# Attention with block summaries and two MLPs on one core: second batch's v means from one product, first heads whole, a new order and engine table

## The chip, the cores and the metric

The kernel runs on one core of one Trainium2 chip, as one program. The metric is the device time of that core in microseconds (us). Three runs of the kernel before took 600.23, 600.83 and 600.94 us, a median of 600.83. Five engines work side by side: TensorE (PE, with its weight loads as PEld), VectorE (DVE), ScalarE (ACT), GpSimd (POOL) and SyncE (SP), which here only issues transfers. Each runs its own list of instructions in order and waits on semaphores for the others.

## What is computed

```
q, k, v: (2, 8, 768, 64)         block, window = 32, 16
k_sum = max  of k over each block of 32 tokens      -> (B, H, 24, D)
v_sum = mean of v over each block of 32 tokens      -> (B, H, 24, D)
scores_l = q k^T / 8, masked to |i - j| < 16
scores_s = q k_sum^T / 8 + log(32)
a   = softmax over [scores_l, scores_s]
out = a @ [v, v_sum]                                -> x: (1536, 512)
x   = MLP 1: h = x @ w_in (512 x 2048), g = rational(h), x = g @ w_out
out = MLP 2: h = x @ w_in (512 x 2048), g = h cos(h),    out = g @ w_out
```

The weights come as 64-bit floats and are converted on the chip.

## The kernel before

The tokens of both batches are cut into 12 units of 128 tokens, six for each batch. A unit u goes through three steps. `attn_a` gathers the 96 keys of each half's window beside the 24 block maxima into a tile `kw` (in `room`), makes the scores of all 8 heads in two PSUM tiles (`sp`, 16 products of 120 columns), and then does the softmax head pair by head pair: DVE adds the mask and finds the maximum (line 656), ACT takes the exponential (660), DVE inverts the sums (670), POOL or DVE scales (673). `attn_b` transposes the scaled scores (`ptp`, line 687) and copies them out (`pt`). `attn_c` multiplies them with a tile `vw` that holds 96 rows of v and 24 rows of block means (`avp`, line 734); its result becomes two halves of x (`xH`, and `xL` on line 745).

The block means of v are a product too. Tokens are loaded with 2 per partition, DVE or POOL adds the pairs, and a product with the selector `vsel` (1/32 where a partition belongs to a block) sums the rest. A batch has 768 tokens, so it takes 3 loads, 3 additions and 3 products of 512 columns that add up in one PSUM bank (`vmp`): `v_mean0` (lines 507, 514, 517) for batch 0 and `v_mean1` (loads of `raw`, lines 539 and 542) for batch 1. The result is copied to `big`, and four small transfers (line 719) bring it to the four `vw`.

Batch 0's keys come as 8 loads into `part` and are transposed by products (`ktp`, line 463); each is copied (327) and reduced to maxima (471). The queries of units 0 and 1 come as two loads, one for each 4 heads, and are transposed in halves (`qtp`, line 432). For units 0 and 1 `attn_a` works head pair by head pair: four gathers, four groups of 4 products, each with its own waits.

The MLPs follow in the same stream of PE work: `h` products (864, later 962), elementwise work on ACT, DVE and POOL, `acc` products (1106). Weight tiles of 512 KB come into `raw`, a pool of 3 buffers that `v_mean1` shares, and DVE converts each with three instructions (760, 764, 768), the last of which frees the buffer. Their loads all start at line 415.

The order is fixed. `Plan.op` records every operation with the engines that may run it, and `Plan.order` reads the packed table `ORDER`, which gives the place of each operation in one long list and its engine. Every engine gets its operations in that sequence, and SP its transfers. PSUM has 4 shared banks (`ps`) and 4 accumulators (`acc0` to `acc3`, used early for transposes).

Of the kernel before, what the change touches and what calls it, by code (L numbers as in the profile page):

```python
# [35 lines left out]
for _p, _t in (("AA", .143), ("AP", .17), ("AT", .25), ("AV", .14), ("PA", .08), ("PP", .08), ("PT", .15),  # L36
# [20 lines left out]
    "c-rk)ON?g6RsQOA-*w;jf4}<g{`)o4-P7Zq=^1+-9?wi>?7=wWB#vccTP8ROa%>aJ1|csTD`5dy#8QX>i%1qqK!CD{;t"  # L57
    "+(8B3OY4Qp5_0B|FwE*dTFk)xEbTSwz6PtN-r*KB~^+JKs5{sv+FasgQC63MdEQF^-Fy3?2?-dffr`rQ~1-$In5*agKK"
    "P57-&k`|Y{do&Zb5F~_gT=?vlcRZ+5_?~j0?E?gY!IH~l<s?;B1UKL`F0`eH%5ZANt0$7PXEnM*sR~{H}mI<6w-*>?BU"
    "w4xwmORI7%gcCzc#wUS>jW~_#U#^V`a~lC>24UnzonvA;c_U3vv1$SRovaZeVJXy^`Cy~^7auPd1?!nzJ6uv@y&<NZ+`"  # L60
    "8Mw>ED=A3eIk&ttiDaG*BVw$I@F;>PaIx39muxxd(Y=ffW@HdYHP=iglW=6rGZjrshU!{-h@eK^1J)ZxJ;>_7368{+8j"
    ";MSXm&dxp_+y1F~VQ}RqJI|~Bz0Y2LM!ga|T|Iqw?QV7VBG$@s?fO*Ct8sCCRP10l$glL5`LcI>+{@=xKAj$y<^JJ442"
    "v6sb9=~xtzMO2RSc6Kt}pU9E@x@~;ZeNX8$zF1@9S!JQQShgm`$%0FJ5&gSr!hCqgxkK#9{Hc#z7R^O2XaUca;9zPVn+"
    "p^l0R7JpZRF1n$~7S3bSkd}@AX-`(4t&1Ro~bL%Z^+<cSYxcBykb1fFvL>3L>FGhL%imPtCER!-(;%xSs*cCfa{A(X<d"
    "g8s5_j%-%-1A5L?PpzGI68Qv;K_hXeaHXH@@B+^P~KIcxqE>hE%+By@KrAu&v@`c>GHvEMcR8f{LCf~qoI10$!O&sF4<"
    "IUs)<-%jThqm#g6mLXzPn?_B;HQ1^=%R=d2j@er2!s8J4|G4El1h`^K5#e2&%n{=aR;>)6(d|JYjm%PQWO|2q~5J|7(c"
    "!GA7334h=*jEZvb&&U;IMnrlfj=_n}=lu!?z>~Lg=Mkh^Th7g^|A0qVa3X=r9J2rsyud+NIS#x?UI>q3In*8iAG^qyix"
    "ohc_#rr4?9#L!QvwP64RLw?SHQ;~<KrLb+xY%1Y=18VR)3D_&)6s3?@(qqA2|ysJ-ZDV4j_VlZ4)x2xEx22tOu`p%)3!"
# [173 lines left out]
def pool(n):  # L242
    return Shared(0.2 + n * 0.00207)
# [7 lines left out]
def kernel(  # L251
# [92 lines left out]
    NQ, NVW = 2, 4  # L344
    NKW = 2
# [154 lines left out]
    def v_mean0(lead):  # L500
# [3 lines left out]
        for i in range(3):  # L504
# [11 lines left out]
            P.op([("T", 0.89)], [raw], [vp],  # L516
# [12 lines left out]
    def v_mean1(lead):  # L529

        kr = kT[1]
        o2 = NP * S + NP * NB
        vp = psum([128, NH, D], "vmp")
        for i in range(3):
            raw = load([128, NH, 2 * D], F32, "raw", "raw", 3,
                       v[1, :, 256 * i:256 * i + 256, :].rearrange("h (s j) d -> s h (j d)", j=2),
                       lambda t: t, 1.75, P.now - lead)
            P.op([("P", pool(512)), ("V", dve2(512))], [], [raw],
                 lambda e, raw=raw: E[e].tensor_tensor(
                     out=raw.t[:, :, 0:D], in0=raw.t[:, :, 0:D], in1=raw.t[:, :, D:2 * D], op=ALU.add))  # L540
            P.op([("T", 0.89)], [raw], [vp],
                 lambda e, i=i, raw=raw: nc.tensor.matmul(  # L542
                     out=vp.t[WK:KW], lhsT=vsel[:, 16 - 8 * i:40 - 8 * i], rhs=raw.t[:, :, 0:D],
                     start=i == 0, stop=i == 2))
        P.op([("A", act(512, True)), ("V", dve(512))], [vp], [kr["v"]],
             lambda e: cp(e, kr.t[WK:KW, o2:o2 + NH * D].rearrange("p (h d) -> p h d", h=NH), vp.t[WK:KW]))
        P.now += 2.7
# [3 lines left out]
    def q_tile(u, lead):  # L551
        b, t = divmod(u, UPB)
        tp = psum([128, NP, 128], "qtp", u < 2)
        if u == 0:
            for i in range(2):
# [6 lines left out]
                     prio=P.now - lead)  # L562
        dst = qTs[u % NQ]
        if u < 2:
            for i in range(2):
                def tr(e, i=i):
                    for x in range(2):
                        transpose_pairs(tp.t[:, 2 * i + x, :], q_first[i][1]()[:, 2 * x:2 * x + 2], 64 * u, 64)

                P.op([("T", 0.44)], [q_first[i][0]], [tp[i], dst[i]], tr)  # L570
                P.op([("A", act(256, True)), ("V", dve(256))], [tp[i]], [dst[i]],
                     lambda e, i=i: cp(e, dst.t[:, 2 * i:2 * i + 2], tp.t[:, 2 * i:2 * i + 2]))
            P.now += 0.88
            return
        raws = [load([128, NH, D], F32, "qk", "qk", 3,
                     q[b, :, 128 * t:128 * t + 128, :].rearrange("h s d -> s h d"), lambda t: t, 1.3,
                     P.now - lead)]

        def tr(e):
            for pr in range(NP):  # L580
                nc.tensor.transpose(tp.t[:, pr, :], raws[0].t[:, 2 * pr:2 * pr + 2], ident)

        P.op([("T", 0.44)], raws, [tp, dst[0], dst[1]], tr)
        P.op([("A", act(512, True)), ("V", dve(512))], [tp], [dst[0], dst[1]], lambda e: cp(e, dst.t, tp.t))
        P.now += 0.44

    def win(u):

# [738 lines left out]
```

## Time and profile before

| what | us |
|---|---|
| median of 3 runs | 600.83 |
| the profiled execution, whole | 601.26 |
| its span in the trace | 599.4 |
| PE busy | 585.9 (98%) |
| DVE busy | 548.4 (92%) |
| ACT busy | 434.1 (72%) |
| POOL busy | 304.3 (51%) |

The whole time is 1.9 us more than the span of the engines' work. The granted TensorE clock is 1.00 in every stretch. An engine's busy share is an average over unlike stages: the attention units lie in the first sixth of the span, beside the first products of MLP 1, and after that come only MLP units. The end of the program is set by the last `acc` products and their output.

### The profile page before, as it was taken

The page shows a single profiled execution, that of the slowest core. Times are in us where ns is not written, and L with a number is a line of the kernel's source. Part 1 is how long each engine was busy: PE and PEld are TensorE (multiplying, and loading weights), DVE is VectorE, ACT ScalarE, POOL GpSimd, SP SyncE. Part 2 cuts the span into 40 slices and gives each one's busy share as a digit, 9 for nine tenths or more (in the row PEclk, how much of TensorE's full clock was granted, in tenths as well). Part 3 has the DMA queues.
Part 4 walks back from the last instruction along what each step waited for, and adds up shares of the span by engine and source line. Part 5 has one row for each costly group of instructions (what it writes and reads, how often), then busy time and mean ns, then how long its engine had stood idle before and what let it go on. Part 6 is the DMA issues. An engine that isn't in the chain of part 4 may idle for free.

```text
span 599.4 us, 10933 instructions
## 1 busy us (share of the span) xinstructions
PE 585.9 (98%) x3897; PEld 501.0 (84%) x3897; DVE 548.4 (92%) x1119; ACT 434.1 (72%) x954; POOL 304.3 (51%) x303
## 2 busy tenths in 40 slices
PE   8879999999999999999999999999999999999997
PEld 7568878888888888888888888888989989998996
DVE  4999999979999999998999999999999998887874
ACT  3989999877587756876789897766767566554653
POOL 5587975247537564557577542444355423732130
PEclk9999999999999999999999999999999999999999
DMA  9897874200321313311220112123322331100104
GB/s 264 218 258 192 204 209 120 75 0 2 106 71 37 106 36 105 106 52 56 70 71 1 36 36 71 37 71 104 109 71 70 106 108 36 35 1 1 53 1 158
DMA packets 68862, 51.85 MB, mean 87 GB/s; under 512 B 37304, under 2 KB 63160, under 8 KB 68808
## 3 DMA queue, kind: packets, MB, share of 16 engines
q1 hardware_dynamic: 68664, 51.03, 29.0%
q8 instruction: 30, 0.49, 0.3%
q14 instruction: 24, 0.20, 0.1%
q10 hardware_dynamic: 144, 0.13, 0.1%
HBM read 47.71 MB, written 3.15 MB: 85 GB/s over the span
## 4 chain that ended last, share of the span: by engine, by line
PE 87%; DVE 9%; ACT 2%; DMA 1%; issue 0%; POOL 0%; SPq 0%; POOLq 0%; DVEq 0%; ACTq 0%
PE acc L1106 43%; PE h L864 22%; PE h L962 18%; DVE sc L656 2%; DMA vw<-in_v_dram 1%; PE avp L734 1%; DVE f L764 1%; DVE f L768 1%; PE ptp L687 1%; PE sp L626 1%; PE warm L356 1%; PE ktp L463 1%; DVE f L760 1%; PE vmp L542 0%; DVE big L471 0%
## 5 line engine op out<-in xcount | busy, mean ns | idle before, releaser
L1106 PE MATMUL acc<-gh,w 128*128 128x512 f32 (+1 forms) x416 | 123.1, 378 | 0.0
L1106 PE MATMUL acc<-w,gh 128*128 128x512 f32 x382 | 119.3, 394 | 0.0
L864 PE MATMUL h<-xH,w 128*128 128x512 f32 (+1 forms) x320 | 99.1, 371 | 0.1
L777 POOL TENSOR_TENSOR gl<-te,gh 128x512 fp32r<-128x512 f32 (+1 forms) x48 | 62.7, 1307 | 67.2 <-ACT gh L322 33.5
L1106 PEld LDWEIGHTS acc<-gh,w 128*128 128x128 f32 x416 | 75.3, 188 | 14.9 <-issue 1.5
L1106 PE MATMUL acc<-gl,w 128*128 128x512 f32 (+1 forms) x208 | 77.6, 373 | 0.0
L1106 PEld LDWEIGHTS acc<-w,gh 128*128 128x128 f32 x382 | 66.7, 189 | 9.4
L1106 PE MATMUL acc<-w,gl 128*128 128x512 f32 x191 | 74.3, 389 | 0.0
L1023 POOL TENSOR_TENSOR tu<-tu,tf 128x512 f32<-128x512 f32 (+1 forms) x41 | 51.4, 1255 | 41.2 <-ACT tf L1015 40.9
L777 POOL TENSOR_TENSOR w<-f,w 128x512 fp32r<-128x512 f32 x39 | 54.4, 1397 | 29.5 <-ACT w L322 15.0
L864 PEld LDWEIGHTS h<-xH,w 128*128 128x128 f32 x320 | 58.5, 188 | 10.6 <-DVE big L495 0.3
L864 PE MATMUL h<-xL,w 128*128 128x512 f32 (+1 forms) x160 | 58.9, 368 | 0.0
L864 PE MATMUL h<-big,w 128*128 128x512 f32 x216 | 52.0, 389 | 0.0
L768 DVE SCALAR_TENSOR_TENSOR f<-raw,f 128x512 int32<-128x512 int32 x64 | 48.3, 759 | 0.3
L1013 ACT ACTIVATE tu<-h,co 128x512 f32<-128x512 f32 (+1 forms) x52 | 33.9, 652 | 19.3 <-PE h L864 18.2
L764 DVE SCALAR_TENSOR_TENSOR f<-raw,f 128x512 int32<-128x512 int32 x64 | 47.3, 745 | 0.6
L864 PEld LDWEIGHTS h<-big,w 128*128 128x128 f32 x216 | 40.6, 188 | 8.4
L1106 PEld LDWEIGHTS acc<-gl,w 128*128 128x128 f32 x208 | 39.1, 188 | 7.0
L1106 PEld LDWEIGHTS acc<-w,gl 128*128 128x128 f32 x191 | 35.9, 188 | 7.9
L1057 ACT ACTIVATE tu<-te 128x512 int32<-128x512 f32 x27 | 17.1, 632 | 32.5 <-DVE te L987 32.2
L324 POOL TENSOR_SCALAR w<-f 128x512 fp32r<-128x512 f32 x28 | 20.0, 715 | 39.8 <-DVE f L768 35.1
L1033 ACT ACTIVATE h<-tf 128x512 f32<-128x512 f32 (+1 forms) x52 | 29.6, 570 | 12.0 <-DVE te L1027 10.8
(222 smaller groups left out, 1530.9 us busy)
## 6 DMA issues: line engine op xcount, KB each, us to landing
raw<-in_moe_w_in_dram SPq DMA_DIRECT2D x32, 512.0 KB, 4.6
raw<-in_moe_w_out_dram SPq DMA_DIRECT2D x32, 512.0 KB, 3.4
vw<-in_v_dram SPq DMA_DIRECT2D x24, 192.0 KB, 3.5
qk<-in_q_dram SPq DMA_DIRECT2D x10, 256.0 KB, 5.3
out_dram<-part SPq DMA_DIRECT2D x8, 256.0 KB, 2.8
part<-in_k_dram SPq DMA_DIRECT2D x8, 192.0 KB, 4.8
big<-in_v_dram SPq DMA_DIRECT2D x3, 512.0 KB, 6.7
qk<-in_k_dram SPq DMA_DIRECT2D x6, 256.0 KB, 5.4
```

The costliest lines, as they stand in the source:

```text
L324: nc.gpsimd.tensor_scalar(out=o, in0=i, scalar1=1.0, scalar2=1.0, op0=ALU.mult, op1=ALU.mult)
L656: lambda e, pr=pr, hh=hh, sv=sv, sp=sp: nc.vector.tensor_tensor_reduce(out=sv()[:, pr, :], in0=sp.t[:, pr, :], in1=m.t, op0=ALU.add, op1=A ...
L764: lambda e: nc.vector.scalar_tensor_tensor(out=ft.t.bitcast(I32), in0=lohi()[1], scalar=-0x40000000, in1=ft.t.bitcast(I32), op0=ALU.bitwis ...
L768: lambda e: nc.vector.scalar_tensor_tensor(out=ft.t.bitcast(I32), in0=lohi()[0], scalar=29, in1=ft.t.bitcast(I32), op0=ALU.logical_shift_r ...
L777: lambda e: E[e].tensor_tensor(out=lo(), in0=x(), in1=hi().bitcast(F32), op=ALU.subtract),
L864: nc.tensor.matmul(out=h.t[:, 0:n], lhsT=lt, rhs=rt[:, kk, cs], start=(k0 == 0 and i == 0), stop=(k0 == 2 and i == 5))
L962: nc.tensor.matmul(out=bank.t[:, c], lhsT=lt, rhs=rt, start=start and i == 0, stop=stop and i == 5, skip_group_check=True)
L1013: lambda e: nc.scalar.activation(out=U(), in_=H(), func=ACTF.Square, scale=b1s))
L1023: lambda e: E[e].tensor_tensor(out=U(), in0=U(), in1=Z(), op=ALU.add))
L1033: lambda e: nc.scalar.activation(out=H(), in_=Z(), func=ACTF.Exp, scale=-1.0))
L1057: lambda e: nc.scalar.activation(out=K().bitcast(I32), in_=S_(), func=ACTF.Identity, scale=1.0 / (2.0 * math.pi)))
L1106: nc.tensor.matmul(out=dst, lhsT=lt, rhs=rt, start=(un.start and not have and i == 0), stop=(un.stop and i == 2), skip_group_check=have)
```

## The change

It has three parts beside a new table.

- Batch 1's means: 4 loads of 96 partitions, each partition with 8 tokens of which a load brings 2. The pairs of each load are added, the second to fourth results are added to the first, and one product over 96 partitions with a rebuilt selector gives all 24 blocks. The selector is rebuilt on POOL after batch 0's products. The first load's `raw` buffer is held until that product.
- The heads of units 0 and 1 are whole: one transpose step and one copy for each unit's queries, one gather, one group of 16 score products, as for the other units. All keys are loaded and transposed first.
- `ORDER` gives a new sequence and new engines for operations all over the kernel.

```diff
     def v_mean1(lead):
...
-        for i in range(3):
+        def eighths(e):
+            sel = vsel[:, 0:24]
+            nc.gpsimd.memset(sel, 1.0 / 32.0)
...
+        P.op([("P", 0.6)], [], [vsel_r], eighths)
+        first = None
+        for i in range(4):
             raw = load([128, NH, 2 * D], F32, "raw", "raw", 3,
-                       v[1, :, 256 * i:256 * i + 256, :].rearrange("h (s j) d -> s h (j d)", j=2),
-                       lambda t: t, 1.75, P.now - lead)
+                       v[1].rearrange("h (s j) d -> s h (j d)", j=8)[:, :, 2 * D * i:2 * D * i + 2 * D],
+                       lambda t: t[0:NW8], 1.13, P.now - lead)
...
             P.op([("P", pool(512)), ("V", dve2(512))], [], [raw],
...
-            P.op([("T", 0.89)], [raw], [vp],
-                 lambda e, i=i, raw=raw: nc.tensor.matmul(
-                     out=vp.t[WK:KW], lhsT=vsel[:, 16 - 8 * i:40 - 8 * i], rhs=raw.t[:, :, 0:D],
-                     start=i == 0, stop=i == 2))
+            if first is None:
+                first = raw
+                continue
+            P.op([("P", pool(512)), ("V", dve2(512))], [raw], [first],
+                 lambda e, raw=raw: E[e].tensor_tensor(out=pair(first), in0=pair(first), in1=pair(raw), op=ALU.add))
+        P.op([("T", 0.89)], [first, vsel_r], [vp],
+             lambda e: nc.tensor.matmul(out=vp.t[WK:KW], lhsT=vsel[0:NW8, 0:24], rhs=pair(first),
+                                        start=True, stop=True))
...
-        if u < 2:
-            for y in every:
-                gather([y])
-        else:
-            gather(list(every))
...
+        P.op([("T", SPT)], [qt, kw["s"], kw["w"]], sps, mm)
...
-            fill.append((k_pair, 0, 30.0))
-            fill.append((q_tile, 0, 30.0))
-            for i in range(1, NP):
+            for i in range(NP):
                 fill.append((k_pair, i, 30.0))
...
 ORDER = (
-    "c-rk)ON?g6RsQOA-*w;jf4}<g{`)o4-P7Zq=^1+-9?wi>?7=wWB#vccTP8ROa%>aJ1|csTD`5dy#8QX>i%1qqK!CD{;t"
+    "c-rk*ON=DhRlV;M|9@mgM1Cr>GApyPva7m2{h98e+#`4Ocs~6x<3VnZ2KS8ZvD<iTFm6WO78b%10wl{a2-}R2EQH1y11"
...
```

PE's first rows before: transposes of keys and queries alternate, and score products (`sp`; the numbers are buffers) stand among them.

```order
L463 MATMUL ktp<-ident,part 64x128 x12
L432 MATMUL qtp<-ident,part 64x64 x16
L463 MATMUL ktp<-ident,part 64x128 x30
L432 MATMUL qtp<-ident,part 64x64 x8
L626 MATMUL sp_290<-room,qT_214 64x120
L626 MATMUL sp_292<-room,qT_214 64x120
...
L463 MATMUL ktp<-ident,part 64x128 x6
```

PE's first rows now.

```order
L465 MATMUL ktp<-ident,part 64x128 x48
L434 MATMUL qtp<-ident,part 64x64 x32
L646 MATMUL sp_308<-room,qT_305 64x120
L646 MATMUL sp_310<-room,qT_305 64x120
...
L519 MATMUL vmp<-big,vsel 24x512 x3
L597 MATMUL qtp<-ident,qk 128x128 x4
L692 MATMUL ptp<-ident,sc 120x128 x4
```

The same 48 and 32 transposes and 32 score products stand there, in three blocks instead of eight.

PE around one of batch 1's three products of means before; one more stands ahead of these rows and one behind them.

```order
L1106 MATMUL acc_992<-gl,w_724 128x256
L542 MATMUL vmp<-raw,vsel 24x512
L1106 MATMUL acc_812<-gh,w_724 128x256 x2
...
L687 MATMUL ptp<-ident,sc 120x128 x4
L1106 MATMUL acc_1032<-gh,w_724 128x256 x2
L1106 MATMUL acc_1032<-gl,w_724 128x256
L581 MATMUL qtp<-ident,qk 128x128 x4
```

PE around the one product now.

```order
L692 MATMUL ptp<-ident,sc 120x128 x8
L597 MATMUL qtp<-ident,qk 128x128 x4
L1111 MATMUL acc_930<-gh,w_1055 128x256 x2
L1111 MATMUL acc_930<-gl,w_1055 128x256
L597 MATMUL qtp<-ident,qk 128x128 x4
L563 MATMUL vmp<-raw,vsel 24x512
L646 MATMUL sp_1467<-room,qT_305 64x120
```

Two products are gone, and the two groups of transposes of the seventh unit (`ptp`) stand together ahead of the one that is left.

SP's first transfers before.

```order
L454 DMA part<-in_k_dram 128x2x192 x2
L559 DMA part<-in_q_dram 128x4x128
L454 DMA part<-in_k_dram 128x2x192
L559 DMA part<-in_q_dram 128x4x128
L454 DMA part<-in_k_dram 128x2x192 x5
L507 DMA big<-in_v_dram 128x8x128 x3
L415 DMA qk<-in_q_dram 128x8x64
```

SP's first transfers now.

```order
L456 DMA part<-in_k_dram 128x2x192 x8
L417 DMA raw<-in_v_dram 96x8x128
L579 DMA part<-in_q_dram 128x4x128 x2
L509 DMA big<-in_v_dram 128x8x128 x3
L382 DMA co<-in_moe_a_dram 128x4
L417 DMA qk<-in_q_dram 128x8x64
```

The first of batch 1's four loads of v stands ahead of the first queries.

DVE now, behind the seventh unit's scores (`sp_1274`, `sp_1276`); rows that read out the maxima stand between these.

```order
L661 ISA sc,mn<-sp_1274,room 128x120
...
L555 TENSOR_TENSOR raw<-raw 96x8x64
L561 TENSOR_TENSOR raw<-raw 96x8x64
L750 TENSOR_TENSOR xL_110<-avp,xH_109 128x4x128
...
L782 TENSOR_TENSOR gl<-te,gh 128x256
L555 TENSOR_TENSOR raw<-raw 96x8x64
L561 TENSOR_TENSOR raw<-raw 96x8x64 x2
```

Of the seven additions for batch 1's means five stand on DVE; before, one of three did, and POOL had two, as it has now.

## Rows read from the trace of the kernel before

**Rows 1.** Windows: busy PE, PEld, DVE, ACT, POOL; clock, DMA, GB/s

```profile
0.00:20.00 20.00, 16.85 (x244) 13.66 (x244) 11.09 (x45) 9.28 (x35) 11.25 (x39) 1.00 0.94 262
20.00:40.00 20.00, 15.92 (x223) 12.07 (x222) 19.77 (x78) 19.33 (x75) 12.95 (x14) 1.00 0.87 218
40.00:60.00 20.00, 18.31 (x234) 16.43 (x235) 20.00 (x74) 18.97 (x67) 15.25 (x19) 1.00 0.81 219
60.00:80.00 20.00, 19.29 (x216) 16.27 (x215) 19.54 (x69) 18.35 (x62) 17.88 (x19) 1.00 0.89 232
80.00:100.00 20.00, 19.94 (x273) 16.23 (x271) 18.85 (x80) 19.05 (x73) 12.74 (x15) 1.00 0.57 153
100.00:120.00 20.00, 20.00 (x181) 16.21 (x179) 18.55 (x45) 16.62 (x41) 6.45 (x6) 1.00 0.26 71
```

**Rows 2.** Timeline of PE, batch 1's products: start, us, line, [idle before <-releaser]

```profile
73.53 1.02 PE L542 MATMUL vmp<-raw,vsel 128*24 128x512 f32 x2 [0.60 <-DVE mn L656]
74.48 1.05 PE L626 MATMUL sp<-room,qT 64*64 64x120 f32 x32
```

**Rows 3.** Timeline of PE, the head

```profile
5.14 2.33 PE L463 MATMUL ktp<-ident,part 128*64 128x128 f32 x24
7.39 0.68 PE L432 MATMUL qtp<-ident,part 64*64 64x64 f32 x16
9.28 3.58 PE L463 MATMUL ktp<-ident,part 128*64 128x128 f32 x60
...
17.49 0.88 PE L626 MATMUL sp<-room,qT 64*64 64x120 f32 x16 [1.03 <-ACT room L322]
...
25.14 1.15 PE L734 MATMUL avp<-pt,vw 120*64 120x64 f32 x30 [0.51 <-ACT pt L322]
```

**Rows 4.** Timeline of DVE, first and last of an unbroken run of scores

```profile
17.00 0.27 DVE L656 CUSTOM_DVE_ANT_0 sc<-sp,room 128x120 f32<-128x120 f32 x1
...
20.11 0.28 DVE L656 CUSTOM_DVE_ANT_0 sc<-sp,room 128x120 f32<-128x120 f32 x1
```

**Rows 5.** Groups of DVE by line and form: xcount | busy us, mean ns

```profile
L471 DVE TENSOR_REDUCE big<-ktp 128x12 f32<-128x384 f32 x8 | 4.1, 547 | 0.3 <-ACT big L322 0.3
L327 DVE COPY big<-ktp 128x384 f32<-128x384 f32 x4 | 2.2, 555 | 8.4 <-PE ktp L463 8.3
L514 DVE TENSOR_TENSOR big<-big 128x512 f32<-128x512 f32 x1 | 1.5, 1514 | 0.0
L539 DVE TENSOR_TENSOR raw<-raw 128x512 f32<-128x512 f32 x1 | 0.9, 887 | 0.0
```

**Rows 6.** Timeline of PE, transposes of the eighth and the ninth unit

```profile
82.11 0.65 PE L687 MATMUL ptp<-ident,sc 128*120 128x128 f32 x4
85.29 0.60 PE L687 MATMUL ptp<-ident,sc 128*120 128x128 f32 x4
88.51 0.60 PE L687 MATMUL ptp<-ident,sc 128*120 128x128 f32 x4
```

**Rows 7.** Timelines of DVE and POOL, the scalings that those wait for

```profile
80.31 0.66 DVE L673 TENSOR_TENSOR sc<-sc,su 128x480 f32<-128x480 f32 x1
83.21 0.99 POOL L673 TENSOR_TENSOR sc<-sc,su 128x480 f32<-128x480 f32 x1
86.70 0.99 POOL L673 TENSOR_TENSOR sc<-sc,su 128x480 f32<-128x480 f32 x1
```

**Rows 8.** Window of DVE alone: length, busy, clock, DMA share, GB/s

```profile
72.00:84.00 12.00, 11.23 (x65) 1.00 0.81 225
```

**Rows 9.** DMA issues: size, median us from issue to landing

```profile
raw<-in_moe_w_in_dram SPq DMA_DIRECT2D x32, 512.0 KB, 4.6
raw<-in_moe_w_out_dram SPq DMA_DIRECT2D x32, 512.0 KB, 3.4
big<-in_v_dram SPq DMA_DIRECT2D x3, 512.0 KB, 6.7
```

More of the change, by code (lines that the diff above doesn't have):

```diff
@@ L533, in v_mean1 @@
         vp = psum([128, NH, D], "vmp")
-        for i in range(3):
+        def eighths(e):
+            sel = vsel[:, 0:24]
+            nc.gpsimd.memset(sel, 1.0 / 32.0)
+            nc.gpsimd.affine_select(out=sel, in_=sel, pattern=[[-4, NB]], compare_op=ALU.is_ge, fill=0.0, base=0,
+                                    channel_multiplier=1)
+            nc.gpsimd.affine_select(out=sel, in_=sel, pattern=[[4, NB]], compare_op=ALU.is_ge, fill=0.0, base=3,
+                                    channel_multiplier=-1)
@@ L546, in v_mean1 @@
              lambda e: cp(e, kr.t[WK:KW, o2:o2 + NH * D].rearrange("p (h d) -> p h d", h=NH), vp.t[WK:KW]))
-        P.now += 2.7
+        P.now += 0.9
     q_first = []
@@ L562, in q_tile, with tr @@
                      prio=P.now - lead)
-        dst = qTs[u % NQ]
-        if u < 2:
[L565 to L584, printed above, removed]
+        if u < 2:
+            raws = [x for x, _ in q_first]
+            def tr(e):
+                for pr in range(NP):
+                    h0 = 2 * (pr % 2)
+                    transpose_pairs(tp.t[:, pr, :], q_first[pr // 2][1]()[:, h0:h0 + 2], 64 * u, 64)
+        else:
+            raws = [load([128, NH, D], F32, "qk", "qk", 3,
+                         q[b, :, 128 * t:128 * t + 128, :].rearrange("h s d -> s h d"), lambda t: t, 1.3,
+                         P.now - lead)]
+            def tr(e):
+                for pr in range(NP):
+                    nc.tensor.transpose(tp.t[:, pr, :], raws[0].t[:, 2 * pr:2 * pr + 2], ident)
+        dst = qTs[u % NQ]
+        P.op([("T", 0.88 if u < 2 else 0.44)], raws, [tp, dst], tr)
+        P.op([("A", act(512, True)), ("V", dve(512))], [tp], [dst], lambda e: cp(e, dst.t, tp.t))
         P.now += 0.44
@@ L641, in attn_a, with windows @@
-        if u < 2:
-            for y in every:
-                gather([y])
-        else:
-            gather(list(every))
+        if t < NKW:
+            P.op([("P", Shared(0.6)), ("A", act(192))], [kr[x] for x in kr.subs if x[0] == "s"], [kw["s"]],
+                 lambda e: cp(e, kw.t[:, :, :, WK:KW],
+                              ks().unsqueeze(2).to_broadcast([128, NP, 2, NB])))
+        def windows(e):
+            if ws[1] - ws[0] == 64:
+                x = kk()[:, :, ws[0]:ws[0] + 128].rearrange("p n (a s) -> p n a s", a=2)
+                x = bass.AP(x.tensor, x.offset, [x.ap[0], x.ap[1], x.ap[2], [1, WK]])
+                cp(e, kw.t[:, :, :, 0:WK], x)
+            else:
+                for half in range(2):
+                    cp(e, kw.t[:, :, half, 0:WK], kk()[:, :, ws[half]:ws[half] + WK])
@@ new lines, in attn_a, with mm @@
+        n = 768
+        P.op([("P", Shared(0.85)), ("A", act(n)), ("V", dvef(n))], sorted(kks, key=id), [kw["w"]], windows)
+        def mm(e):
+            for pr in range(NP):
+                for half in range(2):
+                    for hh in range(2):
+                        p0, c0 = 64 * hh, 64 * half
+                        nc.tensor.matmul(out=sps[hh].t[c0:c0 + 64, pr, :],
+                                         lhsT=qt.t[p0:p0 + 64, pr, c0:c0 + 64],
+                                         rhs=kw.t[p0:p0 + 64, pr, half, :], start=True, stop=True)
```

141 lines of the change are left out of this document (58 added, 83 removed).

## The prediction

> **What bounds the kernel now.** I read the windows first, then PE's timeline, then the other engines' timelines where PE waits. The windows say that the kernel has two lives [rows 1]. From 100 us on PE is busy 20.00 of 20 us, and the end of the program is PE's remaining work laid end to end; the page's first part agrees (98% over the span). Ahead of that PE stands still: 20 less the busy time is 3.15, 4.08, 1.69, 0.71 and 0.06 us in the first five windows, 9.69 us together. There DVE has the work: 19.77, 20.00 and 19.54 of 20 us, with ACT close behind at 19.33, 18.97 and 18.35. So a microsecond of PE work that is removed counts in full only where PE is the engine that others wait for, and from 20 to about 75 us it is not: there DVE and ACT decide when PE's next scores and transposes may start. The granted clock is 1.00 (2.4 GHz) in every window, in the head too, so no term stands for it.
>
> **Batch 1's means on PE.** Two of three products of 512 columns go. Each occupies PE from 73.53 to 74.48, when the next product starts: 0.95 us [rows 2], so 1.9 us for two. They stand between 73.5 and 81 us, just where PE stops waiting: the first of them itself waited 0.60 us for DVE's scores [rows 2]. What is late next are the transposes of the following units, which need scores that were scaled. They start at 82.11, 85.29 and 88.51 us [rows 6]; the scalings end at 80.31 + 0.66 = 80.97, 83.21 + 0.99 = 84.20 and 86.70 + 0.99 = 87.69 [rows 7]. PE could therefore come 1.14, 1.09 and 0.82 us earlier and no more, as long as DVE, ACT and POOL do not come earlier too. Of the 1.9 us the smallest, 0.82, is kept, and the rest turns into a wait. Bounds: all of 1.9 if those engines move along; nothing if they fall behind by 0.8.
>
> **The head.** The same transposes and score products are issued, in three blocks. Walked with the rows: the first 24 key instructions run from 5.14 to 7.39, the other 72 at 3.58/60 = 0.060 us each to 11.7, 64 of the queries at 0.68/16 = 0.043 us to 14.4 [rows 3], and the scores, 32 instructions in about 1.0 us [rows 2], end at 15.4 for unit 0 and 16.4 for unit 1. Before, the last of them ended at 17.49 + 0.88 = 18.4 [rows 3], since the groups waited in between (1.03 us in the row). The extra transfer ahead of the queries, 96 x 8 x 128 x 4 bytes = 0.39 MB at 262 GB/s [rows 1], puts them 1.5 us later; they are now needed at 11.7 instead of 7.4, which covers it. DVE can begin its unbroken run of scores at about 15.5 instead of 17.00 [rows 4], and unit 0's `avp` comes about 1 us earlier than 25.14 [rows 3].
>
> That microsecond is DVE's to give, and DVE gives it back. Up to 15.5 it has 8 reductions, 3 copies and the copy of one unit's queries: 8 x 0.47 + 3 x 0.46 + 0.6 = 5.7 us by the durations [rows 5] less some 0.08 of overlap each, so it stands idle 9.8 us; before, it was idle 20 - 11.09 = 8.9 us in its first window and busy from then on [rows 1]. What it need no longer do ahead of the seventh unit's last score is the addition of 1.51 us and one copy of 0.55 [rows 5], with two small window copies; against that come a whole gather, two casts of weights and a subtraction that the table moved ahead. By the order and the mean durations the net is some 0.8 us less. So 0.9 more idle, 0.8 less work: the seventh unit's scores end where they did, and I count the head as zero. Bounds: 1.0 us gained, if ACT, which drops a dozen small copies, was the one that mattered; 0.9 lost, if the removed DVE work was hidden.
>
> **Batch 1's means on DVE.** Five of the seven additions go to DVE where one did: 4 x 0.887 = 3.5 us more [rows 5]. Two stand behind the seventh unit's scores, three behind the eighth's, and only the ninth's queue behind all of them. Counted to its last score, moved work included, DVE has about 1.1 us more ahead than before. In 72 to 84 us it was idle 12 - 11.23 = 0.77 [rows 8]; that takes up most, and 0.3 us comes off the 0.82. POOL keeps two additions and gets a memset and two selects for the selector, ahead of nothing that waits; with 12.74 busy of 20 us [rows 1] it covers them.
>
> The SBUF — State Buffer page of the Trainium skill (Who interferes with whom) says that a DVE instruction with two SBUF inputs and a GpSimd instruction that reads SBUF block each other for a whole instruction. Row and rule go together in one case: the same addition took 1.514 us beside POOL's additions and 0.887 elsewhere [rows 5]. By the rule every one of the five might pay that difference, which makes a rival below.
>
> **The table beyond 100 us.** The order changes in every stretch, but PE's work there is the same, DVE gets some 10 us less and POOL about 20 us more over the whole kernel, and PE has no idle time to lose or win. I put it at nothing, with up to 1 us of new waits as the bound.
>
> **The sum.** -0.82 (two products, as far as PE can use them) + 0 (head) + 0.1 (part of the 0.3 that DVE is late, since PE may fill it with `acc` work that stands ready) = -0.7 us. The profiled execution took 601.26 us, its span of 599.4 and 1.9 around it, so it would take 600.5; it lies 0.4 above the median of the three runs, and the median goes from 600.83 to 600.1.
>
> **Rivals.**
> - All of it is kept (faster). ACT, not DVE, sets the seventh to ninth unit; it has about 2 us less work ahead of them, so the scaled scores come earlier and PE keeps 1.9 us: 600.83 - 1.9 = 598.9, and 597.9 with the head's 1.0 us. For it: ACT's 19.05 of 20 us in the fifth window [rows 1]. Against: DVE's 20.00 in the third. Chance 0.37.
> - The held buffer (slower). One of three `raw` buffers now holds batch 1's first load from the head until the product, so weight tiles have two. A load can start only when the tile two before it is converted. In DVE's order about 4.5 us of work stand between the two events for the third weight tile and 3.4 for the eighth; the loads take 4.6 (w_in) and 3.4 (w_out) by the median [rows 9], which costs next to nothing. In the head a load of the same size took 6.7 [rows 9]. From about 0.7 us over the median it decides: at 1.2 over, DVE waits 1.3 + 1.2 = 2.5 us ahead of the seventh unit, all passes on to PE, and the time is 600.1 + 2.5 = 602.6. Chance 0.13.
> - The five additions are blocked by POOL (slower). Each takes 1.51 instead of 0.89 us: 3.1 more on DVE, ahead of the ninth unit. Less the 0.8 that PE can take, that is +2.3 on 600.1: 602.4. For it is the one row at 1.514; against, the other at 0.887, and POOL's idle 7 us in the fifth window. Chance 0.07.
>
> **How the numbers follow.** My own case, 600.1, has 0.43. A measurement of this kernel can tell 0.2% (1.2 us) from no change, and this case lies within it. Faster by more than that has the first rival's 0.37; slower has 0.13 + 0.07 = 0.20. The range must reach into both: 598.2 holds about two thirds of the first rival, 602.2 leaves out most of the other two.
>
> **What would show it.** In the trace after, `avp` of unit 0 starts near 24 us and the run of scores near 15.5; the seventh unit's scores end within 0.5 us of 73.5; PE shows new waits of some 1 us in all before transposes between 75 and 92 us; DVE's additions take about 0.9 us. PE's busy time falls by 1.9 us and its idle time grows by about 1.2. I am wrong if PE's idle time up to 100 us stays at 9.7 or less (first rival), if DVE shows idle time released by a `raw` transfer (second), or if the additions take 1.5 us (third).

## The result and the profile after

The changed kernel takes 604.29 us (median of 6 runs, 603.19 to 608.89) where the kernel before took 600.88 (6 runs): a ratio of 1.0058, 95% interval 1.0035 to 1.0081, so it is 0.58% or 3.5 us slower by the ratio. The prediction had 600.1 and a range up to 602.2. In a second set of runs the ratio was 1.0068 (1.0046 to 1.0090). Two of the six executions, at 605.62 and 608.89 us, had a lower mean granted TensorE clock (0.994 and 0.992) and lie above the other four.

The profiled execution took 603.43 us with a span of 601.7. PE's busy time fell from 585.9 to 583.3 us, as the two products and a little more are gone; DVE's from 548.4 to 546.2; POOL's rose from 304.3 to 325.6. Here are the windows of the changed kernel, columns as in [rows 1]:

```profile
0.00:20.00 20.00, 17.16 (x249) 14.03 (x250) 10.57 (x46) 9.03 (x31) 13.64 (x37) 1.00 0.93 258
20.00:40.00 20.00, 14.95 (x224) 11.94 (x221) 19.51 (x74) 18.69 (x69) 14.71 (x17) 1.00 0.94 238
40.00:60.00 20.00, 17.28 (x230) 15.59 (x231) 19.86 (x73) 18.42 (x67) 15.09 (x19) 1.00 0.70 191
60.00:80.00 20.00, 17.03 (x201) 14.90 (x199) 17.92 (x66) 17.82 (x60) 10.72 (x12) 1.00 0.70 174
80.00:100.00 20.00, 18.93 (x271) 15.44 (x272) 19.26 (x85) 18.89 (x75) 11.30 (x12) 1.00 0.67 176
100.00:120.00 20.00, 20.00 (x178) 16.22 (x177) 18.18 (x46) 16.66 (x42) 10.99 (x10) 1.00 0.39 118
```

PE stands idle for 2.84, 5.05, 2.72, 2.97 and 1.07 us in the first five windows, 14.65 together where it was 9.69 [rows 1]: 0.3 less than before in the first window and 1.0, 1.0, 2.3 and 1.0 more in the next four. The 5.0 us more of idle time outweigh the 2.6 us less of work, which gives the 2.3 us between the two spans but for rounding, and from 100 us on PE is full in both. So the loss lies in the first 100 us. From 60 to 80 us DVE, too, works 17.92 us where it worked 19.54: something holds DVE itself.

PE's timeline of the head (start, us, line, [idle before <-releaser]) answers to [rows 3], and the first score on DVE to [rows 4]:

```profile
14.13 1.87 PE L646 MATMUL sp<-room,qT 64*64 64x120 f32 x64 [0.26 <-ACT room L323]
...
24.17 1.15 PE L739 MATMUL avp<-pt,vw 120*64 120x64 f32 x30 [0.28 <-ACT pt L323]
...
29.03 0.66 PE L597 MATMUL qtp<-ident,qk 128*128 128x128 f32 x4 [0.82 <-DMA qk<-in_q_dram]
```

```profile
15.35 0.28 DVE L661 CUSTOM_DVE_ANT_0 sc<-sp,room 128x120 f32<-128x120 f32 x1 [0.73 <-PE sp L646]
```

Scores begin at 15.35 instead of 17.00 and unit 0's `avp` at 24.17 instead of 25.14, as forecast. New is the row at 29.03: PE waits 0.82 us for the fourth unit's q tile (the expectations below call it the third unit's, or the third q tile). That tile's transfer was issued at 24.65 us, before at 25.01; PE comes to it at 28.21 instead of 29.36, so here it is PE that is earlier and not the transfer that is issued later.

The next rows lie at 69 to 78 us: transfers issued on SP (start, time of the issue), then DVE's timeline.

```profile
68.82 1.66 SPq L417 DMA_DIRECT2D raw<-in_v_dram  x2
...
77.15 0.31 SPq L417 DMA_DIRECT2D raw<-in_v_dram  x1
```

```profile
69.42 0.69 DVE L773 SCALAR_TENSOR_TENSOR f<-raw,f 128x512 int32<-128x512 int32 x1
...
73.48 0.28 DVE L661 CUSTOM_DVE_ANT_0 sc<-sp,room 128x120 f32<-128x120 f32 x1
...
75.66 0.69 DVE L555 TENSOR_TENSOR raw<-raw 96x512 f32<-96x512 f32 x1 [1.88 <-DMA raw<-in_v_dram]
76.43 0.69 DVE L561 TENSOR_TENSOR raw<-raw 96x512 f32<-96x512 f32 x1
...
77.64 0.16 DVE L675 RECIPROCAL su<-su 128x4 f32<-128x4 f32 x1
77.73 0.25 DVE L661 CUSTOM_DVE_ANT_0 sc<-sp,room 128x120 f32<-128x120 f32 x1
```

Four transfers of `v` go into a pool of three `raw` buffers. The first, from the head, is added in last, and it keeps its buffer until that addition (not until the product, as the section on the change has it). The second and third are issued as a pair, each when a weight tile's last conversion frees a buffer; the third therefore has to wait for the conversion at 69.42. DVE ends the seventh unit's last score at 73.8, reaches the pair addition of the third load, and stands for 1.88 us, since DVE works in order and the data is not there. The fourth is issued at 77.15, when the addition at 76.43 gives its buffer back. Behind the waiting addition stand the seventh unit's reciprocals and the eighth unit's scores. The chain of work that ended last runs through it (start, us, what):

```profile
70.14 5.49 DMA raw<-in_v_dram
...
75.66 0.70 DVE raw L555
```

The transfer's 5.49 us are the longest piece of the chain in this stretch. POOL and PE pass the wait on:

```profile
72.59 1.29 POOL L555 TENSOR_TENSOR raw<-raw 96x512 f32<-96x512 f32 x1 [0.39 <-DVE mn L661]
77.89 1.99 POOL L678 TENSOR_TENSOR sc<-sc,su 128x480 f32<-128x480 f32 x2 [4.01 <-DVE su L675]
```

```profile
78.93 0.65 PE L692 MATMUL ptp<-ident,sc 128*120 128x128 f32 x4 [1.67 <-POOL sc L678]
80.07 0.62 PE L692 MATMUL ptp<-ident,sc 128*120 128x128 f32 x4 [0.49 <-DVE mn L661]
...
83.01 1.02 PE L563 MATMUL vmp<-raw,vsel 96*24 96x512 f32 x2 [0.99 <-ACT sc L665]
```

POOL stands 4.01 us for a reciprocal, PE 1.67 us for the scaling behind it and 0.49 and 0.99 more. The transposes at 78.93 and 80.07 are the seventh unit's. In the kernel before, PE's timeline has these two groups earlier and without a wait:

```profile
77.80 0.60 PE L687 MATMUL ptp<-ident,sc 128*120 128x128 f32 x4
...
79.17 0.62 PE L687 MATMUL ptp<-ident,sc 128*120 128x128 f32 x4
```

### The profile page after: what moved, and what is told of

It reads as the page before. It is cut to its first block, busy times and chain, and to the rows that moved or that the text cites. A ratio compares the mean times of both kernels' runs of the same rounds, so it can differ in the third digit from the quotient of the medians.

```text
span 601.7 us, 10895 instructions
## 1 busy us (share of the span) xinstructions
PE 583.3 (97%) x3893; PEld 500.3 (83%) x3893; DVE 546.2 (91%) x1101; ACT 435.2 (72%) x945; POOL 325.6 (54%) x320
## 4 chain that ended last, share of the span: by engine, by line
PE 86%; DVE 8%; DMA 3%; issue 1%; ACT 1%; SPq 1%; DVEq 0%
PE acc L1111 42%; PE h L869 23%; PE h L967 18%; DVE sc L661 1%; PE avp L739 1%; DMA part<-in_q_dram 1%; PE ptp L692 1%; DMA raw<-in_v_dram 1%; PE sp L646 1%; DMA qk<-in_q_dram 1%; DVE f L773 1%; DVE f L769 1%; SPq L456 1%; DVE big L497 1%; DVE tu L1040 0%
## 5 line engine op out<-in xcount | busy, mean ns | idle before, releaser
L782 POOL TENSOR_TENSOR gl<-te,gh 128x512 fp32r<-128x512 f32 (+1 forms) x56 | 73.0, 1305 | 58.4 <-ACT gh L323 38.7
L1028 POOL TENSOR_TENSOR tu<-tu,tf 128x512 f32<-128x512 f32 (+1 forms) x45 | 56.6, 1260 | 35.0 <-ACT tf L1020 34.0
L773 DVE SCALAR_TENSOR_TENSOR f<-raw,f 128x512 int32<-128x512 int32 x64 | 49.8, 787 | 0.4
L769 DVE SCALAR_TENSOR_TENSOR f<-raw,f 128x512 int32<-128x512 int32 x64 | 47.3, 744 | 0.5
L1069 ACT ACTIVATE h<-h 128x512 f32<-128x512 f32 x48 | 28.0, 583 | 20.2 <-DVE h L1066 20.0
L1035 ACT ACTIVATE tf<-tu 128x512 f32<-128x512 f32 (+1 forms) x52 | 31.1, 599 | 12.9 <-POOL tu L1028 12.0
L665 ACT ACTIVATE sc<-sc,mn 128x120 f32<-128x120 f32 x96 | 36.9, 388 | 3.7 <-DVE mn L661 3.7
```

The source lines that it names most:

```text
L665: lambda e, pr=pr, hh=hh, sv=sv: nc.scalar.activation(out=sv()[:, pr, :], in_=sv()[:, pr, :], func=ACTF.Exp, scale=-1.0, bias=mn.t[:, hh, ...
L769: lambda e: nc.vector.scalar_tensor_tensor(out=ft.t.bitcast(I32), in0=lohi()[1], scalar=-0x40000000, in1=ft.t.bitcast(I32), op0=ALU.bitwis ...
L773: lambda e: nc.vector.scalar_tensor_tensor(out=ft.t.bitcast(I32), in0=lohi()[0], scalar=29, in1=ft.t.bitcast(I32), op0=ALU.logical_shift_r ...
L782: lambda e: E[e].tensor_tensor(out=lo(), in0=x(), in1=hi().bitcast(F32), op=ALU.subtract),
L1028: lambda e: E[e].tensor_tensor(out=U(), in0=U(), in1=Z(), op=ALU.add))
L1035: lambda e: nc.scalar.activation(out=Z(), in_=U(), func=ACTF.Ln, bias=QC))
```

## Experiments

Theory 1: the held buffer makes the next loads of `v` late (the expectations call each of batch 1's four loads an eighth), and DVE's wait in order costs the time. Theory 2: DVE's four more additions cost it, whatever the loads do. Theory 3: the new order and the whole heads cost it. Theory 4 came up on the way: the 0.39 MB in the head make a q tile late, and PE's wait for it is followed by a lower clock. "Low clock" counts executions whose mean granted clock was under 0.998; the kernel before had 12 of 87.

| kernel | median us (runs) | ratio to before, 95% | low clock | median of the others |
|---|---|---|---|---|
| after, first set | 604.29 (6) | 1.0058 [1.0035, 1.0081] | 2 | 603.76 |
| a_again | 606.08 (6) | 1.0068 [1.0046, 1.0090] | 4 | 604.50 |
| b_noprod | 600.30 (11) | 0.9990 [0.9981, 0.9999] | 1 | 600.19 |
| e_nowait | 602.84 (6) | 1.0036 [1.0022, 1.0050] | 1 | 602.35 |
| e_oneadd | 602.83 (12) | 1.0028 [1.0009, 1.0046] | 5 | 602.35 |
| e_freed2 | 602.91 (12) | 1.0021 [1.0004, 1.0038] | 5 | 601.56 |
| e_late | 602.52 (12) | 1.0026 [1.0009, 1.0043] | 6 | 601.19 |
| e_all | 601.18 (12) | 1.0001 [0.9990, 1.0012] | 2 | 601.06 |
| b_head | 603.16 (12) | 1.0026 [1.0008, 1.0044] | 8 | 600.63 |
| a_q | 605.38 (5) | 1.0072 [1.0056, 1.0089] | 2 | 605.38 |
| e_q | 602.46 (11) | 1.0024 [1.0011, 1.0038] | 4 | 602.08 |
| e_best | 604.02 (7) | 1.0047 [1.0029, 1.0065] | 7 | - |
| e_pool | 607.02 (6) | 1.0078 [1.0053, 1.0103] | 6 | - |
| e_freed, e_part | 609.18, 608.12 (5, 5) | 1.0125, 1.0120 | 5, 5 | - |

**The products alone (b_noprod).** The kernel before, without two of its three products (they are issued for i = 2 only), so their share of the means is left out.

```diff
-                 lambda e, i=i, raw=raw: nc.tensor.matmul(
+                 lambda e, i=i, raw=raw: i == 2 and nc.tensor.matmul(
```

> The kernel before without the first two of the three products for batch 1's means (the means of tokens 0 to 511 are left out); everything else stays. It prices the term of the sum for the two products alone. The prediction's step: 0.82 of 1.9 us kept, 600.88 - 0.8 = 600.1. Rival (PE is what others wait for): all 1.9 kept, 599.0. Rival (PE waits there anyway): 600.9.

Measured: 0.6 us less (0.06 to 1.1). PE's waits in this stretch:

```profile
77.21 0.65 PE L687 MATMUL ptp<-ident,sc 128*120 128x128 f32 x4 [0.58 <-POOL sc L673]
...
78.88 0.62 PE L687 MATMUL ptp<-ident,sc 128*120 128x128 f32 x4 [0.23 <-DVE mn L656]
```

These transposes wait 0.58 us for POOL's scaling and 0.23 for DVE, where the kernel before had no wait (77.80 and 79.17 above). Most of the 1.9 us was not saved, and waits for the other engines appear, as the prediction's step had it; but they stand ahead of the seventh unit's transposes and not ahead of the later ones at 82.11 to 88.51 [rows 6] that the step went by. Those start without a wait here too.

**The wait alone (e_nowait).** DVE's first two additions read a load that has landed; one load is left out of the means.

```diff
+            if i == 1:
+                raw = first
             P.op([("P", pool(512)), ("V", dve2(512))], [], [raw],
```

> The changed kernel, but DVE's first two additions of batch 1's means add halves of the eighth that landed before (so these means are other numbers); the transfer that DVE waited 1.88 us for is issued as before and nobody reads it. Same work on DVE, same transfers, same order; only the wait is gone. Theory 1: DVE goes on at 73.8 instead of 75.66 us, the eighth unit's scores and both reciprocals come 1.9 us earlier, PE's wait of 1.67 us before the transposes shrinks, and the time is 604.3 - 1.9 = 602.4. Theory 2 (the work itself): 604.3 within 0.5.

DVE's timeline at the same place:

```profile
73.86 0.28 DVE L663 CUSTOM_DVE_ANT_0 sc<-sp,room 128x120 f32<-128x120 f32 x1
...
74.15 0.69 DVE L557 TENSOR_TENSOR raw<-raw 96x512 f32<-96x512 f32 x1
...
76.17 0.25 DVE L663 CUSTOM_DVE_ANT_0 sc<-sp,room 128x120 f32<-128x120 f32 x1
```

The addition starts right behind the last score, the eighth unit's scores come at 76.17 instead of 77.73, and PE's wait of 1.67 us is gone from its timeline: at 78.51 it waits 0.44.

```profile
78.51 0.62 PE L694 MATMUL ptp<-ident,sc 128*120 128x128 f32 x4 [0.44 <-DVE mn L663]
```

The time falls to 602.84, close to the 602.4 that theory 1 named. DVE's work is the same, so theory 2 has no part in these 1.5 us. The intervals of the two ratios (1.0022 to 1.0050 here, 1.0035 to 1.0081 in the first set) overlap, so this run alone does not fix the size; the rows show the mechanism.

**The buffer (e_freed, e_part, then e_freed2).** The head's load goes into the unused end of the tile with batch 0's `v`, its pair sum into `part`.

```diff
-            raw = load([128, NH, 2 * D], F32, "raw", "raw", 3,
+            if i == 3:
+                end = View(vroom[0], lambda t: t[:, 3072:4096].rearrange("p (h x) -> p h x", h=NH))
+                raw = View(early_room(0), lambda t: t[:, 0:512].rearrange("p (h d) -> p h d", h=NH))
```

> The changed kernel, but the eighth of v that is loaded in the head goes into 4 KB per partition that nobody uses then (the end of the tile with the first batch's v), and its pair sum into 2 KB of a tile that is free after the head; so no raw buffer is held, and orders and engines stay. Theory 1 (a held buffer makes the next loads late, and DVE waits for one in order): the two loads at 68.82 and 70.14 us come one freed buffer earlier, some 2.4 and 1.3 us, DVE's wait of 1.88 us falls to about 0.5, and the time to 602.4 to 603.0 from 604.3. Theory 2 (DVE's four more additions and the new table cost it, whatever the loads do): 604.3 within 0.5.

> The changed kernel, but all four eighths lie outside the raw buffers: the head's as in the run that frees a buffer, the others in the two tiles of the first k and q, which stand unused from 14 to 94 us, and their three transfers are issued some 20 us earlier, between 39 and 62 us. The additions keep engines and places. Theory 1: DVE waits for no v at all (2.2 us less), 604.3 - 2.2 = 602.1; if weight tiles with three buffers give something in 20 to 60 us too, under 602. Theory 2: 604.3 within 0.5.

Both missed, through the edit and not the theory: the sum was placed ahead of the products that read the keys in those columns, so the keys were overwritten and PE had to wait for the sum. e_freed's windows show it (columns as in [rows 1]):

```profile
8.00:12.00 4.00, 0.00 (x0) 0.00 (x0) 1.02 (x2) 0.03 (x1) 0.12 (x1) 1.00 1.04 285
12.00:16.00 4.00, 2.81 (x26) 2.81 (x28) 0.00 (x0) 0.48 (x1) 1.14 (x1) 0.55 1.01 292
16.00:20.00 4.00, 4.00 (x54) 3.83 (x52) 3.07 (x6) 0.83 (x2) 2.09 (x4) 0.60 1.12 287
```

PE does nothing from 8 to 12 us, and the granted clock is 0.55 and 0.60 (part of the time at 1.2 GHz) while it works again. In e_freed2 the sum is issued behind those products.

> The changed kernel with the head's eighth outside the raw buffers (its load at the same place, into 4 KB that are free then; its pair sum into a tile whose first columns PE has read by then), so that three raw buffers are there for all else; orders and engines as in the changed kernel. Theory 1 (held buffer): the two loads of v come 1.3 and 2.4 us earlier, DVE's wait of 1.88 falls to 0.5 or less, 604.3 - 1.5 = 602.8. Theory 2 (DVE's additions): 604.3.

SP and DVE:

```profile
67.58 2.45 SPq L417 DMA_DIRECT2D raw<-in_v_dram  x2
...
73.99 0.58 SPq L417 DMA_DIRECT2D raw<-in_v_dram  x1
```

```profile
74.66 0.69 DVE L562 TENSOR_TENSOR raw<-raw 96x512 f32<-96x512 f32 x1
...
79.39 0.68 DVE L562 TENSOR_TENSOR raw<-raw 96x512 f32<-96x512 f32 x1
```

The pair is issued 1.2 us earlier and the fourth load at 73.99 instead of 77.15, with no addition to wait for. DVE's additions start without idle time, and its list of waits in 20 to 100 us has no transfer of `v` left. 602.91 against a_again's 606.08 on the same chip, with intervals of the ratios that do not touch: theory 1 stands. At full clock it is 601.56 against 604.50.

> The changed kernel once more, on the same chip as the runs beside it. All theories: 604.3, between 603.2 and 605.5; if its time were 602 or less here, the wait of 1.88 us would be no cause of its own and a difference of chips.

a_again was somewhat slower than expected, with four of six executions at a mean clock of 0.994; more on that below.

**DVE's additions (e_oneadd).** Four of the five are left out, so two loads are missing from the means.

```diff
-                 lambda e, raw=raw: E[e].tensor_tensor(
+                 lambda e, raw=raw, i=i: i in (1, 2) or E[e].tensor_tensor(
```

> The changed kernel, with the last of DVE's five additions left in (so the head's buffer is held just as long) and the other four left out, so the means miss two of four eighths; the four loads are issued, two are read by nobody. It takes away the wait and 4 x 0.69 = 2.8 us of DVE's work. Theory 1 (the wait alone): as the run without the wait, 602.8. Theory 2 (DVE sets the pace up to the ninth unit, so its added work counts in full, and PE's saved products count only then): 602.8 - 2.5 = 600.3. Theory 3 (the new order and whole heads cost what is left): 602.8.

602.83: the same as without the wait, with 2.8 us less on DVE. Theory 2 falls; in this order DVE's additions cost nothing that could be measured once their data is there (e_best, below, shows what they fill).

**All additions on POOL (e_pool).** The additions become POOL's and move ahead, for example `put(496, 381, 'P')`.

> The changed kernel with all four eighths outside the raw buffers (three loads some 20 us earlier, between 39 and 57 us), and all seven additions on POOL in places where it stood idle; DVE has none. The whole reference is computed. Theories 1 and 2 together: the wait (1.9) and 3.45 us of DVE's work go, 600.0 (599.5 to 600.8), at or below the kernel before. Theory 3 (order and whole heads): 602.5 or more.

A clear miss: 607.02. DVE's timeline (three instructions of a weight tile's conversion are lines 775, 779, 783), then POOL's:

```profile
67.61 0.41 DVE L775 TENSOR_SCALAR f<-raw 128x512 int32<-128x512 int32 x1
...
68.27 0.68 DVE L779 SCALAR_TENSOR_TENSOR f<-raw,f 128x512 int32<-128x512 int32 x1
...
71.05 0.97 DVE L775 TENSOR_SCALAR f<-raw 128x512 int32<-128x512 int32 x1
71.94 1.77 DVE L783 SCALAR_TENSOR_TENSOR f<-raw,f 128x512 int32<-128x512 int32 x1
73.64 1.22 DVE L779 SCALAR_TENSOR_TENSOR f<-raw,f 128x512 int32<-128x512 int32 x1
```

```profile
70.45 1.29 POOL L565 TENSOR_TENSOR part<-part 96x512 f32<-96x512 f32 x1
71.81 1.35 POOL L571 TENSOR_TENSOR part<-part 96x512 f32<-96x512 f32 x1
73.16 1.14 POOL L792 TENSOR_TENSOR gl<-te,gh 128x256 fp32r<-128x256 f32 x1
```

Beside POOL's additions line 775 takes 0.97 instead of 0.41 us and 783 takes 1.77 (the same instruction took 0.69 at 69.42 above); beside POOL's line 792, which is no addition of these means, 779 takes 1.22 instead of 0.68. The seventh unit's scores start at 77.21 instead of 71.34, though 3.3 us of that had come earlier, with a granted clock of 0.57 from 32 to 36 us. It was 0.59 and 0.55 from 76 to 84 us too, and all six executions had the low clock, so 607.02 is not the price of the longer conversions alone. The Trainium skill (SBUF — State Buffer, Who interferes with whom) says that a DVE instruction with two SBUF inputs and a GpSimd instruction that reads SBUF block each other; the rows of lines 779 and 783, with two inputs each, agree; line 775 has one, of which that sentence does not speak. e_all, below, has the same in an addition: DVE's first, no longer waiting for its load, runs beside one of POOL's and takes 1.53 us. In the changed kernel POOL's had ended at 73.88 when DVE's began at 75.66.

**The head's bytes (e_late, e_all, b_head).** Both versions of the changed kernel load into `part`, which no one uses from 14 to 94 us; b_head adds a transfer to the kernel before.

```diff
+                 lambda e, i=i: [i == 1 and nc.sync.dma_start(
+                     out=room.t[0:96, 3072:4096].rearrange("p (h x) -> p h x", h=NH),
...
```

> The changed kernel with the head's eighth loaded some 35 us later (about 39 instead of 4.9 us), into a tile that is free by then, and its pair sum on POOL where it stood idle near 46 us: no held buffer, and 0.39 MB less in the first 30 us, when the DMA engines are full. The rest stays. Theory 4 (beside the held buffer, the 0.39 MB ahead of everything make the third unit's q land late: PE waits 0.8 to 2.2 us for it near 29 us, and where it waits long the granted clock falls to 1.2 GHz for 6 us): that wait goes, the clock stays at 1.00 in nearly all executions, and the time is 602.9 (the run that only freed the buffer) - 1.5 = 601.4, in a band of 1 us instead of 3.5. Theory 1 alone (the held buffer): as the run that only freed the buffer, 602.9 with a band of 3.5 us.

> As the run before it, but all four eighths lie outside the raw buffers and are loaded between 39 and 63 us; the five additions stay on DVE at their places, POOL keeps its two. The whole reference is computed. Theories 1 and 4: DVE waits for no v at all, some 0.5 us less than the run before it, 600.9. If the additions beside POOL's cost DVE its lead again: 601.5 or more. The new order alone would leave it above the kernel before, 601.5.

> The kernel before with one more transfer of 0.39 MB that nobody reads, in the head ahead of the first batch's v (at the place where the changed kernel loads its first eighth); no buffer is held for it and nothing else changes. Theory 4: v and the q tiles of the next units land some 1.3 us later, PE waits near 29 us as in the changed kernel, and the time is 600.9 + 1 = 601.9, with some executions 2 to 3 us longer at a lower clock. Theory 1 alone, and the prediction's step that the transfer is covered: 600.9.

b_head is 1.6 us slower (0.5 to 2.6) by nothing but 0.39 MB. Its windows and PE's timeline:

```profile
28.00:32.00 4.00, 1.77 (x27) 1.25 (x23) 2.63 (x8) 1.26 (x7) 1.18 (x1) 0.77 1.09 345
32.00:36.00 4.00, 3.33 (x40) 3.01 (x40) 2.98 (x20) 3.36 (x14) 2.33 (x3) 0.50 1.04 281
```

```profile
30.90 1.12 PE L583 MATMUL qtp<-ident,qk 128*128 128x128 f32 x4 [2.23 <-DMA qk<-in_q_dram]
32.69 1.88 PE L628 MATMUL sp<-room,qT 64*64 64x120 f32 x32 [0.67 <-ACT qT L322]
```

PE stands 2.23 us for the fourth unit's q tile, which it did not wait for before, and the granted clock falls to 0.50, the level of 1.2 GHz: 32 score products take 1.88 us instead of 1.05 [rows 2]. a_again's profiled execution shows the same, with a wait of 1.59 us:

```profile
28.00:32.00 4.00, 1.73 (x21) 1.19 (x21) 3.19 (x13) 1.97 (x10) 2.31 (x2) 0.68 0.92 254
32.00:36.00 4.00, 4.00 (x44) 3.69 (x36) 2.95 (x20) 2.79 (x13) 2.33 (x2) 0.50 0.63 171
```

```profile
29.85 1.11 PE L597 MATMUL qtp<-ident,qk 128*128 128x128 f32 x4 [1.59 <-DMA qk<-in_q_dram]
```

In the first profile of the changed kernel the wait was 0.82 us and the clock stayed at 1.00; in e_nowait's it was 1.23, with the clock at 1.00 too. b_head's four executions at full clock have a median of 600.63, level with the kernel before, and its other eight one of 604.16: where the clock stays up the transfer is covered, and the loss lies in the executions with the lower clock. But e_late, without those bytes in the head, still had the low clock in 6 of 12, and its profile shows a wait for the same tile:

```profile
28.69 0.65 PE L601 MATMUL qtp<-ident,qk 128*128 128x128 f32 x4 [1.77 <-DMA qk<-in_q_dram]
```

So the 0.39 MB are not the only cause. Nor does the length of a wait settle what the clock does: PE's 1.67 us ahead of 78.93 in the changed kernel left it at 1.00. e_all stands level with the kernel before, with 2 of 12.

**The q tile (a_q, e_q) and the additions' place (e_best).**

```diff
+    put(230, 141)
```

> The changed kernel with one edit: the load of the third q tile that PE waited for near 29 us is issued five places earlier on SP, ahead of the copies of the first means (about 19 instead of 24.65 us). The head's buffer is held as before. Theory 4 in its second form (that tile lands too late for a PE that is earlier, and where PE waits more than about 1.5 us the granted clock falls to 1.2 GHz for some 6 us): no wait for q near 29 us, mean clock 0.998 or more in nearly all executions, 604.2 (the fast part of the changed kernel's executions) with a band of 1.5 us instead of 5. If the clock falls as often as before, the wait for q is not what lowers it. The held buffer alone would leave it at 604.3 to 606.1 with the wide band.

> All four eighths outside the raw buffers and loaded after the head (as the run that came to 601.18), and the third q tile issued five places earlier. Theory 4 in its second form: the wait of 0.5 to 1.8 us for that tile goes, no execution at a lower clock, 600.7. If that wait lay beside the wait for q's copy on ACT anyway: 601.2.

> As the run beside it (eighths outside the raw buffers, q tile earlier), and DVE's first two additions stand behind the eighth unit's last reciprocal instead of ahead of its scores: 1.4 us less ahead of the scalings, for which PE waits 0.54 and 0.49 us at 76 to 78 us. If DVE's place in the order is what is left: 0.8 us less than the run beside it, 600.0. If PE's remaining waits lie elsewhere: the same, 600.7.

All three missed. The wait for q is gone, but at nearly the same time PE waits for a result of DVE, which had waited 0.8 us for a weight tile, and the clock falls again (e_q):

```profile
30.97 0.38 PE L873 MATMUL h<-xL,w 128*128 128x256 f32 x1 [1.59 <-DVE xL L754]
```

```profile
32.00:36.00 4.00, 4.00 (x22) 3.61 (x21) 3.93 (x22) 3.93 (x15) 2.99 (x4) 0.57 0.71 169
```

With the q tile moved ahead another transfer was later: in e_q the weight tile that DVE waited for was issued at 22.69 us, in e_all, without the move, at 21.55. In a_q the median at full clock is 605.38 as well, so there the clock is not what costs the time. In e_best DVE waits for ACT's sums where the additions had stood, and runs the additions later, ahead of the eighth unit's last scores, for which PE waits 2.16 us. So the additions had filled a gap there, which fits that leaving them out gained nothing. PE's 2.16 us left the clock at 1.00. DVE's row, then PE's:

```profile
76.51 0.18 DVE L679 RECIPROCAL su<-su 128x4 f32<-128x4 f32 x1 [1.02 <-ACT su L674]
```

```profile
80.98 0.62 PE L696 MATMUL ptp<-ident,sc 128*120 128x128 f32 x4 [2.16 <-DVE mn L665]
```

No version of the changed kernel beat the kernel before; e_all equals it.

## Why the prediction was wrong

- **The products.** 0.82 us kept of 1.9 was forecast, 0.6 (0.06 to 1.1) measured alone. The size and the kind of wait were right, the place was not: 0.82 is the slack at 88.51, and b_noprod's waits came ahead of the seventh unit's transposes, which the step did not look at. That the two numbers lie so close is in part luck.
- **The head.** The times were right (`avp` near 24, scores near 15.5, the seventh unit's last score within 0.5 us of 73.5: it ended at 73.8). The step "their extra transfer is covered" was right for the queries of the first two units (PE waited 0.17 us for them at 11.96), and in b_head at full clock; it did not follow the transfer, and the earlier PE, on to the fourth unit's q tile, where PE waits and the clock is lower behind it in some executions.
- **Batch 1's means on DVE: the step that failed.** "0.3 us comes off the 0.82" counted the additions as work (0.887 us each; they took 0.69) and not as instructions that wait for a transfer. The second rival had the cause, a held buffer, but looked for its price at the third and eighth weight tiles, where DVE waited for nothing, and gave it a chance of 0.13. The load that came late was one of the change's own four. With two of three buffers tied up, the third load's place in the pool follows from the conversion at 69.42, and 5.49 us of transfer behind that is later than 73.8. The second of the prediction's signs of being wrong, DVE idle time released by a `raw` transfer, is what the trace shows.
- **The third rival.** Additions at 1.51 us did not come: POOL stood idle when DVE added (4.01 us ahead of 77.89). Longer DVE instructions beside POOL's do occur, as e_pool and e_all show.
- **Beyond 100 us.** PE full in both, as forecast. DVE's work over the whole kernel fell by 2.2 us and not by the 10 that the prediction names; its sum does not use that number.
- **The sum.** Forecast: idle time up by 1.2 us; measured: up by 5.0. Taking the held buffer away gives back 0.47% (1.0068 to 1.0021 in one set), some 2.8 us; how much of that is DVE's one wait (1.5 us by e_nowait's median, in another set) was not measured side by side. With the loads also moved, the first out of the head and the others ahead (e_all), nothing of the loss is left, and nothing of the gain has come. What keeps the 0.6 us of the products from showing in e_all is not settled: PE's idle time there is 12.1 us to 100 us, 2.4 more than before, most of it from 40 to 80 us, and the new order was not tried apart from the whole heads. Nor is it settled why low clocks are rarer in e_all than in e_late, with the same head; 2 and 6 of 12 may be chance.

## What to carry to other kernels

When a change keeps a buffer of a shared pool for longer, walk the pool's own list: for each later load the event that frees its buffer, plus the transfer, against the place of its first reader in that engine's order. Do this for the change's own loads first, not only for the tiles that shared the pool before. An engine that works in order turns one late tile into a wait for everything that stands behind it, however little the waiting instruction itself costs.

## What the runs showed of the hardware

- Near 30 us, PE waits of 1.59 us (a_again, e_q), 1.77 (e_late) and 2.23 (b_head) were followed by a granted clock of 0.50 to 0.81 from 32 to 36 us; waits of 0.82 (after) and 1.23 (e_nowait) were not. Waits of 1.67 us ahead of 78.93 (after) and 2.16 us ahead of 80.98 (e_best) were not either, so the runs do not show what decides it. The executions with the lower clock were 1.9 us (a_again) to 3.5 us (b_head) longer by the medians; the wait ahead may be part of that.
- Beside POOL's additions of two SBUF tiles one conversion of DVE took 1.77 us (e_pool), 0.69 without them (after).
- A transfer of 0.39 MB for 96 partitions took 5.49 us from issue to landing at 70 us, longer than the median of 4.6 of a weight tile of 512 KB in [rows 9].
